# A feed-forward output product by Strassen's seven half-size products, with single input buffers

## Chip, cores, metric

The kernel runs on one core of a Trainium2 chip. The metric is the device time of one execution in microseconds (us), as the median of repeated runs. A profiled execution gives a span, from the first to the last instruction, that is some 2 us shorter than the time. The granted clock is the share of TensorE's full clock that its throttle let through, 1 at most.

## The reference

```python
# attention: per head, phi(x) = [relu(x) cos, relu(x) sin], cos and sin by position
kv  = einsum('bhsf,bhsd->bhfd', phi(k), v);   z = sum(phi(k), axis=2)
num = einsum('bhsf,bhfd->bhsd', phi(q), kv)
x   = num / (einsum('bhsf,bhf->bhs', phi(q), z)[..., None] + 1e-6)      # 8 x 8 x 576 x 64
# then, with x as (4608 tokens, 512)
h   = x @ w_in                       # 512 -> 2048
g   = h / (1 + exp(-beta * h))       # beta per column
out = g @ w_out                      # 2048 -> 512
```

## The kernel before

The 4608 tokens go in nine chunks of 512. A chunk has 32 slots. In slots 0 to 15 TensorE makes the sixteen 128-row blocks of h, transposed, and ScalarE turns each into a bfloat16 tile of g. In slots 16 to 31 TensorE makes the output product. The attention of batch c+1 is spread between the slots of chunk c, so that its VectorE and GpSimd work lies beside the matmuls. "h stage" and "output stage" below are these two halves.

```python
raw_pool = tc.tile_pool(name="raw", bufs=2)       # q, k, v of two batches
gt_pool  = tc.tile_pool(name="gt", bufs=20)

def h_bank(c, jt):                                # PSUM bank of an h block; (0, 1, 4, 5) from chunk 2 on
    ...
def h_act(c, jt):
    g_t = gt_pool.tile([P, TCH], BF16, name="g_t", tag="g_t")
    nc.scalar.activation(g_t, ps[:, h_bank(c, jt)], AF.Silu, scale=beta[:, jt : jt + 1])
    gs[c, jt] = g_t

def o_mm(c, tt, jts):                             # 128 tokens x 512 columns, 16 matmuls of N=512
    o_ps = ps[:, (2, 3, 0, 1)[tt] if c == 0 else 2 + tt % 2]
    for jt in jts:
        nc.tensor.matmul(o_ps, lhsT=gs[c, jt][:, tt * P : (tt + 1) * P],
                         rhs=wout[jt // 4][:, jt % 4, :], start=(jt == 0), stop=(jt == JT - 1))
    ...
    nc.scalar.copy(o_sb, o_ps)
    store(c, tt, o_sb)

def att_units(b):                                 # (slot, work) for batch b
    u = [(0, lambda: num_rest() if b == 2 else None),
         (0, lambda: (q_relu(b, 0), q_relu(b, 1), q_turn_dma(b), load_next())),
         (1, lambda: v_scale(b, 0)), (4, lambda: k_relu(b)), (6, lambda: v_scale(b, 1)),   # VectorE
         (7, lambda: q_tan(b, 0)), (8, lambda: q_tan(b, 1)),                               # GpSimd
         (12, lambda: (kv_mm(b, 0, 6), kv_mm(b, 1, 6), kv_take((0, 1), 6)))]
    u.append((18, lambda: (num_all(0, 4), num_all(1, 6), num_all(2, 0))))
    for t, bank in enumerate((4, 6, 0)):
        u.append((18, lambda t=t, bank=bank: (x_div(t, bank), x_turn_dma(b, 3 * t, 3 * t + 3))))
```

kv_mm is a product of k and v into bank 6 and 7, and kv_take is VectorE's copy of it. num_all(t, bank) is a third of the numerators. x_div(t, bank) is VectorE's division of them: a sum, a reciprocal and a multiplication.

## Time and profile before

| | before |
|---|---|
| time, median (range) of three runs | 294.7 us (294.2 to 294.9) |
| span | 292.4 us |
| TensorE, VectorE, ScalarE, GpSimd busy | 97%, 39%, 49%, 26% |
| granted TensorE clock | 0.998 |
| one chunk with attention, TensorE | 30.3 us: h 13.85, kv 1.2, num 1.4, output product 13.85 |

The prediction shows the lines and how they are read.

### The profile page before, as it was taken

To read this page: it belongs to the slowest core of one execution; us is meant where nothing else is said; L and a number is where in the kernel's file an instruction comes from. 1 tells how busy PE (TensorE), PEld (TensorE's weight loads), DVE (VectorE), ACT (ScalarE), POOL (GpSimd) and SP (SyncE) were. 2 spreads that over 40 slices of the span, in tenths; PEclk is the share of its full clock that TensorE was granted. 3 is DMA by queue.
4 is the path that set the end of the run, shared out by engine and by line. 5 is a ranking of instruction groups with operands and counts; after the bars stand their busy time and mean duration, and the time that the engine had idled before them with its cause. 6 is when DMAs were issued, how large, how long until landed. Compare 5 with 4: busy or idle time off the path is not lost.

```text
span 292.4 us, 7218 instructions
## 1 busy us (share of the span) xinstructions
PE 284.0 (97%) x3072; PEld 141.3 (48%) x3072; DVE 114.0 (39%) x287; ACT 142.8 (49%) x228; POOL 74.9 (26%) x89
## 2 busy tenths in 40 slices
PE   7699999999999999999999999999999999999994
PEld 6354455455445544554445444454455444444444
DVE  5889975834900392029301950086005000000000
ACT  5778856862166315721573137412760277137511
POOL 1444000643380038202650265023601210000000
PEclk9999999999999999999999999999999999999999
DMA  6999999999998089907991699139102810131033
GB/s 242 383 389 385 392 349 334 299 264 336 176 284 314 3 159 203 402 34 141 216 392 46 130 217 391 58 65 206 36 2 52 143 36 0 39 83 23 0 74 72
DMA packets 50737, 53.89 MB, mean 184 GB/s; under 512 B 31233, under 2 KB 31633, under 8 KB 50705
## 3 DMA queue, kind: packets, MB, share of 16 engines
q1 hardware_dynamic: 47744, 45.95, 53.8%
q0 software_dynamic: 2688, 7.34, 10.5%
q8 instruction: 24, 0.39, 0.5%
q10 hardware_dynamic: 272, 0.14, 0.2%
q14 instruction: 9, 0.07, 0.1%
HBM read 36.71 MB, written 9.44 MB: 158 GB/s over the span
## 4 chain that ended last, share of the span: by engine, by line
PE 92%; DMA 3%; DVE 2%; SPq 1%; issue 1%
PE ps L365 42%; PE ps L390 42%; PE ps L280 3%; DMA raw_v<-in_v_dram 3%; PE ps L259 3%; PE ps L408 1%; SPq L78 1%; DVE xs L302 1%; PE ps L229 0%; PE ps L339 0%; DVE win L108 0%; DVE rden L295 0%; DVE den L291 0%; DVE rk L189 0%; DVE vb L204 0%
## 5 line engine op out<-in xcount | busy, mean ns | idle before, releaser
L365 PE MATMUL ps<-xt,win 128*128 128x512 bf16 (+1 forms) x580 | 127.3, 378 | 0.1
L390 PE MATMUL ps<-wout,g_t 128*128 128x512 bf16 x560 | 124.4, 379 | 0.0
L372 ACT ACTIVATE g_t<-ps,beta 128x512 bf16<-128x512 f32 x144 | 98.6, 688 | 33.2 <-PE ps L365 33.2
L365 PEld LDWEIGHTS <-win 128*128 128x128 bf16 x580 | 56.0, 98 | 66.0 <-issue 0.5
L390 PEld LDWEIGHTS <-g_t 128*128 128x128 bf16 x560 | 53.7, 98 | 63.9 <-issue 0.3
L385 POOL DMA_DIRECT2D out_dram<-o_sb x56 | 35.9, 645 | 136.7 <-ACT o_sb L396 136.7
L396 ACT COPY o_sb<-ps 128x512 f32<-128x512 f32 x35 | 20.2, 588 | 98.2 <-PE ps L390 94.0
L271 DVE CAST kv<-ps 128x520 bf16<-128x520 f32 x6 | 4.2, 700 | 68.3 <-PE ps L259 68.3
L217 POOL TENSOR_TENSOR qs<-qt,tanr 128x1152 bf16<-128x1152 bf16 x12 | 28.3, 2382 | 8.2 <-DMA qt<-qb 8.2
L411 DVE COPY o_sb<-ps 128x256 f32<-128x256 f32 (+1 forms) x2 | 0.7, 358 | 62.7 <-PE ps L408 62.7
L302 DVE TENSOR_TENSOR xs<-ps,rden 128x768 bf16<-128x768 f32 (+4 forms) x26 | 22.8, 884 | 0.9 <-DVE rden L295 0.2
L291 DVE TENSOR_TENSOR den<-ps,eps 128x12 f32<-128x12 f32 (+4 forms) x26 | 4.1, 159 | 33.6 <-PE ps L280 33.5
L214 DVE TENSOR_SCALAR vb<-raw_v,cos 128x256 bf16<-128x256 f32 x63 | 17.1, 347 | 0.0
L214 DVE TENSOR_SCALAR vb<-raw_v,sin 128x256 bf16<-128x256 f32 x54 | 14.7, 349 | 0.0
L280 PEld LDWEIGHTS <-qt 64*64 64x64 bf16 x576 | 10.4, 106 | 4.9 <-issue 4.5
L259 PE MATMUL ps<-vb,rk 64*64 64x130 bf16 x576 | 10.2, 218 | 2.1 <-ACT rk L187 1.9
L280 PE MATMUL ps<-kv,qt 64*64 64x65 bf16 x576 | 11.7, 195 | 0.5 <-ACT kv L269 0.5
L189 DVE TENSOR_SCALAR qb<-raw_q 128x1152 bf16<-128x1152 f32 x16 | 11.4, 752 | 1.6 <-DMA raw_q<-in_q_dram 1.6
L259 PEld LDWEIGHTS <-rk 64*64 64x64 bf16 x576 | 8.5, 106 | 6.9 <-ACT rk L187 3.6
L280 PE MATMUL ps<-kv,qs 64*64 64x65 bf16 x576 | 11.5, 193 | 0.0
L108 DVE CAST win<-w_stage 64x512 bf16<-64x512 f32 x22 | 10.9, 493 | 1.1 <-DMA w_stage<-in_moe_w_in_dram 0.6
L189 DVE TENSOR_SCALAR rk<-raw_k 128x2304 bf16<-128x2304 f32 (+2 forms) x9 | 10.7, 1186 | 0.6 <-DMA raw_k<-in_k_dram 0.6
(59 smaller groups left out, 98.6 us busy)
## 6 DMA issues: line engine op xcount, KB each, us to landing
raw_v<-in_v_dram SPq DMA_DIRECT2D x7, 1152.0 KB, 10.4
raw_k<-in_k_dram SPq DMA_DIRECT2D x7, 1152.0 KB, 13.6
raw_q<-in_q_dram SPq DMA_DIRECT2D x7, 1152.0 KB, 7.3
out_dram<-o_sb POOLq DMA_DIRECT2D x56, 128.0 KB, 4.4
w_stage<-in_moe_w_in_dram SPq DMA_DIRECT2D x3, 1024.0 KB, 13.4
w_stage<-in_moe_w_out_dram SPq DMA_DIRECT2D x2, 1024.0 KB, 8.0
w_stage<-in_moe_w_out_dram SPq DMA_DIRECT2D x4, 512.0 KB, 12.0
out_dram<-o_sb SPq DMA_DIRECT2D x14, 128.0 KB, 2.3
```

The source lines that it names most:

```text
L108: nc.vector.tensor_copy(o, a)
L189: nc.vector.tensor_scalar(dst, src, scalar1=0.0, scalar2=None, op0=ALU.max)
L214: nc.vector.tensor_scalar(o, a, scalar1=t[:, n : n + 1], scalar2=None, op0=ALU.mult)
L217: eng.tensor_tensor(dst.rearrange("q n (g p) -> q n g p", g=2), src.rearrange("q n (g p) -> q n g p", g=2), tanr[:, n0:n1].unsqueeze(2).to ...
L259: nc.tensor.matmul(t[jj * HP : (jj + 1) * HP, g], lhsT=rk[hs, n, 2 * jp + jj, :], rhs=vb[hs, n, 2 * jp + jj].rearrange("q s e -> q (s e)") ...
L280: nc.tensor.matmul(ps[cols, bank + jj, slot * E : (slot + 1) * E], lhsT=(qt, qs)[cs][rows, jp, n, cols], rhs=kv[rows, g, jp, cs, :], start ...
L302: nc.vector.tensor_tensor(o.rearrange("q j n s d -> q j (n s) d"), nv[:, :, a:z, :, 0:D].rearrange("q j n s d -> q j (n s) d"), rden[:, :, ...
L365: nc.tensor.matmul(ps[:, h_bank(c, jt), blocks.start * 64 : blocks.stop * 64], lhsT=win[jt // 4][:, mi, (jt % 4) * P : (jt % 4 + 1) * P], ...
L372: nc.scalar.activation(g_t, ps[:, h_bank(c, jt)], AF.Silu, scale=beta[:, jt : jt + 1])
L385: eng.dma_start(out=out_v[bb, n][:, m0:m1], in_=o_sb[hf * HP : (hf + 1) * HP, m0:m1])
L390: nc.tensor.matmul(o_ps, lhsT=gs[c, jt][:, tt * P : (tt + 1) * P], rhs=wout[jt // 4][:, jt % 4, :], start=(jt == 0), stop=(jt == JT - 1))
L396: nc.scalar.copy(o_sb, o_ps)
```

## The change

The output product of chunks 1 to 8 is made by a seven-product Strassen scheme. The halves are those of tokens (256 and 256), of d_ff (even and odd 128-blocks) and of d_model. TensorE does an eighth less arithmetic in it, at matmuls of N=256 in place of 512. VectorE makes four sums of g for each chunk (S1 to S4) and four of the weights once (T1 to T4), and puts the products together. The space for these comes from single raw buffers in place of double ones, so loads are issued at other points. In chunk 1, GpSimd makes half of v's scaling. The numerators (num) move from slot 18 to the end of the h stage, so kv_take is needed three slots' matmuls (2.6 us) earlier.

```diff
-    raw_pool = ctx.enter_context(tc.tile_pool(name="raw", bufs=2))
+    raw_pool = ctx.enter_context(tc.tile_pool(name="raw", bufs=1))
...
+    T1, T2, T4 = (const.tile([P, JT // 2, HM], BF16, name=f"T{i}") for i in (1, 2, 4))
+    T3 = B12
+    S1, S2, S3, S4 = (const.tile([P, JT // 2, TCH // 2], BF16, name=f"S{i}") for i in (1, 2, 3, 4))
...
+    def g_sums(c, i0, i1):
...
+        nc.vector.tensor_tensor(s1, A21, A22, op=ALU.add)
+        nc.vector.tensor_tensor(s2, s1, A11, op=ALU.subtract)
+        nc.vector.tensor_tensor(s4, A12, s2, op=ALU.subtract)
+        nc.vector.tensor_tensor(s3, A11, A21, op=ALU.subtract)
+
+    def w_sums(i0, i1):                                   # T1 = B12-B11, T2 = B22-T1, T4 = B21-T2, T3 = B22-B12
...
+    def o_fast(c, pr, b_bank):
+        a_ps, e_ps, b_ps = (ps[:, k_, 0:HM] for k_ in (2, 3, b_bank))
...
+        def s_0():
+            prod(a_ps, g_part(0, 0), B11, True, False)     # 8 matmuls of N=256
+            nc.scalar.copy(p1, a_ps)
+        def s_1():
+            prod(b_ps, s_part(S2), T2, True, False)
+            nc.vector.tensor_tensor(u2, b_ps, p1, op=ALU.add)
...
+        def s_4():
+            prod(b_ps, s_part(S3), T3, False, False)
+            nc.vector.tensor_tensor(o2[:, HM:DM], b_ps, p15, op=ALU.add)
...
+        def s_6():
+            prod(b_ps, g_part(1, 1), T4, False, True)
+            nc.vector.tensor_tensor(o2[:, 0:HM], b_ps, p1, op=ALU.add)
...
         if slot == 24:
-            for name in "qvk":
+            for name in "vkq":
                 load_raw(2, name)
...
+            if slot in (3, 7, 11):
+                g_sums(c, slot // 2 - 1, slot // 2 + 1)
+            elif slot in (13, 15):
+                g_sums(c, slot // 2, slot // 2 + 1)
+            if c == 1 and slot in (5, 9):
+                w_sums(slot - 5, slot - 1)
+        if b < B:
+            num_all(0, 6)
+            num_all(1, 0)
+            num_all(2, 4)
+        x, y = o_fast(c, 0, 6), o_fast(c, 1, 7)            # two pairs of 128 tokens; banks 6 and 7
...
+        x[0]()
+        x_part(0)                                          # the division that reads bank 6
+        x[1]()                                             # the product that writes bank 6
+        x_part(1)
...
+        y[2]()
+        y[3]()
+        if b + 1 < B:
+            v_scale(b + 1, 0)                              # nine VectorE operations
+        y[4]()
+        y[5]()
+        y[6]()
```

x and y are the seven products of the first and the second pair of token blocks. "y4" is the fifth product of the second pair.

More of the change, by code (lines that the diff above doesn't have):

```diff
@@ L58 @@
     small = ctx.enter_context(tc.tile_pool(name="small", bufs=4))
-    gt_pool = ctx.enter_context(tc.tile_pool(name="gt", bufs=20))
+    gt_pool = ctx.enter_context(tc.tile_pool(name="gt", bufs=5))
+    part = ctx.enter_context(tc.tile_pool(name="part", bufs=2))
     osb_pool = ctx.enter_context(tc.tile_pool(name="osb", bufs=4))
@@ L82 @@
     win = [const.tile([P, MI, 512], BF16, name=f"win{i}") for i in range(4)]
-    wout = [const.tile([P, 4, DM], BF16, name=f"wout{i}") for i in range(4)]
+    wout = const.tile([P, JT, DM], BF16, name="wout")
+    HM = DM // 2
+    w_e, w_o = wout[:, 0:JT:2], wout[:, 1:JT:2]
+    B11, B12, B21, B22 = w_e[:, :, 0:HM], w_e[:, :, HM:DM], w_o[:, :, 0:HM], w_o[:, :, HM:DM]
+    T1, T2, T4 = (const.tile([P, JT // 2, HM], BF16, name=f"T{i}") for i in (1, 2, 4))
+    T3 = B12
+    S1, S2, S3, S4 = (const.tile([P, JT // 2, TCH // 2], BF16, name=f"S{i}") for i in (1, 2, 3, 4))
     w_in_v = moe_w_in.rearrange("(j p) f -> p j f", p=P)
@@ L113, in cast_out @@
         if eng == "a":
-            nc.scalar.activation(wout[i][:, jj, :], st[:, jj, :], AF.Copy, scale=rbeta[:, j : j + 1])
+            nc.scalar.activation(wout[:, j, :], st[:, jj, :], AF.Copy, scale=rbeta[:, j : j + 1])
         else:
-            nc.vector.tensor_scalar(wout[i][:, jj, :], st[:, jj, :],
+            nc.vector.tensor_scalar(wout[:, j, :], st[:, jj, :],
                                     scalar1=rbeta[:, j : j + 1], scalar2=None, op0=ALU.mult)
     GJ = [(0, 0), (0, 1), (1, 0), (1, 1)]
-    for name in "qvk":
-        for b in range(2):
-            raw_tile(b, name)
     load_raw(0, "q", 0, 2)
@@ L370, in h_act @@
     def h_act(c, jt):
-        g_t = gt_pool.tile([P, TCH], BF16, name="g_t", tag="g_t")
-        nc.scalar.activation(g_t, ps[:, h_bank(c, jt)], AF.Silu, scale=beta[:, jt : jt + 1])
-        gs[c, jt] = g_t
+        if (c, jt // 4) not in gs:
+            gs[c, jt // 4] = gt_pool.tile([P, 4, TCH], BF16, name="g_t", tag="g_t")
+        nc.scalar.activation(gs[c, jt // 4][:, jt % 4], ps[:, h_bank(c, jt)], AF.Silu, scale=beta[:, jt : jt + 1])
+    def g_sums(c, i0, i1):
+        k_ = i0 // 2
+        g_e, g_o = (gs[c, k_][:, 2 * (i0 - 2 * k_) + r : 2 * (i1 - 2 * k_) : 2] for r in range(2))
+        hf = TCH // 2
+        A11, A12, A21, A22 = g_e[:, :, 0:hf], g_o[:, :, 0:hf], g_e[:, :, hf:TCH], g_o[:, :, hf:TCH]
+        s1, s2, s3, s4 = (t[:, i0:i1] for t in (S1, S2, S3, S4))
+        nc.vector.tensor_tensor(s1, A21, A22, op=ALU.add)
[3 more added lines that the diff above has]
+    def w_sums(i0, i1):
+        a, z = slice(i0, i1), ALU.subtract
+        nc.vector.tensor_tensor(T1[:, a], B12[:, a], B11[:, a], op=z)
+        nc.vector.tensor_tensor(T2[:, a], B22[:, a], T1[:, a], op=z)
+        nc.vector.tensor_tensor(T4[:, a], B21[:, a], T2[:, a], op=z)
+        nc.vector.tensor_tensor(T3[:, a], B22[:, a], B12[:, a], op=z)
     def h_group(c, jt):
@@ L379, with store @@
     out_v = out.rearrange("(b p n) m -> b n p m", b=B, n=NQ)
-    def store(c, tt, o_sb, m0=0, m1=512, two=False):
+    def store(c, tt, o_sb):
         for hf in range(2):
             bb, n = divmod((c * TCH + tt * P) // HP + hf, NQ)
-            eng = (nc.sync, nc.scalar)[hf] if two else nc.sync if c >= 7 else nc.gpsimd
-            eng.dma_start(out=out_v[bb, n][:, m0:m1], in_=o_sb[hf * HP : (hf + 1) * HP, m0:m1])
+            eng = nc.gpsimd if c < 7 else (nc.sync, nc.scalar)[hf] if tt == 3 else nc.sync
+            eng.dma_start(out=out_v[bb, n], in_=o_sb[hf * HP : (hf + 1) * HP])
     def o_mm(c, tt, jts):
@@ L389, in o_mm @@
         for jt in jts:
-            nc.tensor.matmul(o_ps, lhsT=gs[c, jt][:, tt * P : (tt + 1) * P],
-                             rhs=wout[jt // 4][:, jt % 4, :],
+            nc.tensor.matmul(o_ps, lhsT=gs[c, jt // 4][:, jt % 4, tt * P : (tt + 1) * P],
+                             rhs=wout[:, jt, :],
                              start=(jt == 0), stop=(jt == JT - 1))
@@ L400, in o_part, with prod, g_part, at @@
         o_mm(c, tt, range(4 * part, 4 * part + 4))
-    def o_last(c, tt):
-        o_sb = osb_pool.tile([P, DM], FP32, name="o_sb", tag="o_sb")
-        for i, (m0, m1) in enumerate(((0, 256), (256, 384), (384, 512))):
-            o_ps = ps[:, 4 + i, 0 : m1 - m0]
-            for jt in range(JT):
-                nc.tensor.matmul(o_ps, lhsT=gs[c, jt][:, tt * P : (tt + 1) * P],
-                                 rhs=wout[jt // 4][:, jt % 4, m0:m1],
-                                 start=(jt == 0), stop=(jt == JT - 1))
-            (nc.scalar.copy if i == 1 else nc.vector.tensor_copy)(o_sb[:, m0:m1], o_ps)
-            store(c, tt, o_sb, m0, m1, two=True)
+    def o_fast(c, pr, b_bank):
+        a_ps, e_ps, b_ps = (ps[:, k_, 0:HM] for k_ in (2, 3, b_bank))
+        tok = slice(pr * P, (pr + 1) * P)
+        def prod(dst, left, right, start, stop):
+            for i in range(JT // 2):
+                nc.tensor.matmul(dst, lhsT=left(i), rhs=right[:, i], start=start and i == 0,
+                                 stop=stop and i == JT // 2 - 1, skip_group_check=True)
+        def g_part(r, hf):
+            def at(i):
+                jt = 2 * i + r
+                return gs[c, jt // 4][:, jt % 4, hf * (TCH // 2) + pr * P : hf * (TCH // 2) + (pr + 1) * P]
+            return at
+        def s_part(t):
+            return lambda i: t[:, i, tok]
+        o1 = osb_pool.tile([P, DM], FP32, name="o_sb", tag="o_sb")
+        o2 = osb_pool.tile([P, DM], FP32, name="o_sb", tag="o_sb")
+        p1 = part.tile([P, HM], FP32, name="p1", tag="p1")
+        p15 = part.tile([P, HM], FP32, name="p15", tag="p15")
+        u2 = part.tile([P, HM], FP32, name="u2", tag="u2")
+        def s_0():
[4 more added lines that the diff above has]
+            nc.vector.tensor_tensor(u2, b_ps, p1, op=ALU.add)
+        def s_2():
+            prod(e_ps, s_part(S1), T1, True, False)
+            nc.vector.tensor_tensor(p15, e_ps, p1, op=ALU.add)
+        def s_3():
+            prod(a_ps, g_part(1, 0), B21, False, True)
+            nc.scalar.copy(o1[:, 0:HM], a_ps)
+        def s_4():
+            prod(b_ps, s_part(S3), T3, False, False)
+            nc.vector.tensor_tensor(o2[:, HM:DM], b_ps, p15, op=ALU.add)
+        def s_5():
+            prod(e_ps, s_part(S4), B22, False, True)
+            nc.vector.tensor_tensor(o1[:, HM:DM], e_ps, u2, op=ALU.add)
+            store(c, pr, o1)
+        def s_6():
+            prod(b_ps, g_part(1, 1), T4, False, True)
+            nc.vector.tensor_tensor(o2[:, 0:HM], b_ps, p1, op=ALU.add)
+            store(c, pr + 2, o2)
+        return s_0, s_1, s_2, s_3, s_4, s_5, s_6
@@ L564, in num_rest, with att_q, att_h, v_second @@
         x_turn_dma(1, 7, NQ)
-    def att_units(b):
-        def load_next():
-            for name in "qvk":
-                if b + 1 < B:
-                    load_raw(b + 1, name)
-        u = [
-            (0, lambda: num_rest() if b == 2 else None),
-            (0, lambda: (q_relu(b, 0), q_relu(b, 1), q_turn_dma(b), load_next())),
-            (1, lambda: v_scale(b, 0)),
-            (4, lambda: k_relu(b)),
-            (6, lambda: v_scale(b, 1)),
-            (7, lambda: q_tan(b, 0)),
-            (8, lambda: q_tan(b, 1)),
-            (12, lambda: (kv_mm(b, 0, 6), kv_mm(b, 1, 6), kv_take((0, 1), 6))),
-        ]
-        u.append((18, lambda: (num_all(0, 4), num_all(1, 6), num_all(2, 0))))
-        for t, bank in enumerate((4, 6, 0)):
-            u.append((18, lambda t=t, bank=bank: (x_div(t, bank), x_turn_dma(b, 3 * t, 3 * t + 3))))
-        return sorted(u, key=lambda x: x[0])
+    def att_q(b):
+        q_relu(b, 0)
+        q_relu(b, 1)
+        q_turn_dma(b)
+        if b + 1 < B:
+            load_raw(b + 1, "q")
+    def att_h(b):
+        def v_second():
+            if b == 2:
+                for jp in range(2):
+                    v_scale(b, 1, jp, eng="pool")
+            else:
+                v_scale(b, 1)
+            if b + 1 < B:
+                load_raw(b + 1, "v")
+        def k_all():
+            k_relu(b)
+            if b + 1 < B:
+                load_raw(b + 1, "k")
+        return {
+            0: lambda: (num_rest(), att_q(2), v_scale(2, 0)) if b == 2 else None,
+            1: k_all,
+            2: v_second,
+            7: lambda: q_tan(b, 0),
+            8: lambda: q_tan(b, 1),
+            12: lambda: (kv_mm(b, 0, 6), kv_mm(b, 1, 6), kv_take((0, 1), 6)),
+        }
     for slot in range(32):
@@ L602 @@
         if slot == 24:
-            for name in "qvk":
+            for name in "vkq":
                 load_raw(2, name)
@@ L607, with x_part @@
     for c in range(1, NTC):
-        units = att_units(c + 1) if c + 1 < B else []
-        for slot in range(32):
-            if slot < 16:
-                h_group(c, slot)
-            elif c == NTC - 1 and slot >= 28:
-                if slot == 28:
-                    o_last(c, 3)
-            else:
-                o_part(c, (slot - 16) // 4, slot % 4)
-            while units and units[0][0] <= slot:
-                units.pop(0)[1]()
+        b = c + 1
+        units = att_h(b) if b < B else {}
+        for slot in range(16):
+            h_group(c, slot)
+            if slot in units:
+                units[slot]()
+            if slot in (3, 7, 11):
[9 more added lines that the diff above has]
+        x, y = o_fast(c, 0, 6), o_fast(c, 1, 7)
+        banks = (6, 0, 4)
+        def x_part(t):
+            if b < B:
+                x_div(t, banks[t])
+                x_turn_dma(b, 3 * t, 3 * t + 3)
+        x[0]()
+        x_part(0)
+        x[1]()
+        x_part(1)
+        x[2]()
+        x_part(2)
+        x[3]()
+        x[4]()
+        x[5]()
+        if b + 1 < B:
+            att_q(b + 1)
+        y[0]()
+        x[6]()
+        y[1]()
+        y[2]()
+        y[3]()
+        if b + 1 < B:
+            v_scale(b + 1, 0)
+        y[4]()
+        y[5]()
+        y[6]()
 _INS = ['q', 'k', 'v', 'moe_w_in', 'moe_w_out', 'moe_beta']
```

## The prediction

> **What bounds the kernel now.** I began with the page's first two parts. TensorE is busy 97% of the span at full clock, and no other engine is over half.
>
> ```profile
> PE 284.0 (97%) x3072; PEld 141.3 (48%) x3072; DVE 114.0 (39%) x287; ACT 142.8 (49%) x228; POOL 74.9 (26%) x89
> ...
> PEclk9999999999999999999999999999999999999999
> ```
>
> Next the chain of waits that ended last and the table of groups: two matmul lines share the span, the product into d_ff (L365) and the output product (L390), and neither has idle time ahead of it. Per matmul the cost is busy time over count (124.4 / 560 = 0.222 us), not the 379 ns mean, because matmuls overlap.
>
> ```profile
> PE 92%; DMA 3%; DVE 2%; SPq 1%; issue 1%
> PE ps L365 42%; PE ps L390 42%; PE ps L280 3%; DMA raw_v<-in_v_dram 3%; PE ps L259 3%; PE ps L408 1%; SPq L78 1%; DVE xs L302 1%; PE ps L229 0%; PE ps L339 0%; DVE win L108 0%; DVE rden L295 0%; DVE den L291 0%; DVE rk L189 0%; DVE vb L204
> ...
> L390 PE MATMUL ps<-wout,g_t 128*128 128x512 bf16 x560 | 124.4, 379 | 0.0
> ```
>
> Then the timeline of TensorE over one chunk (c=2), columns start, length, engine, line, operation, count:
>
> ```profile
> 81.36 11.39 PE L365 MATMUL ps<-xt,win 128*128 128x512 bf16 x52
> 92.68 1.22 PE L259 MATMUL ps<-vb,rk 64*64 64x130 bf16 x72
> 93.82 2.76 PE L365 MATMUL ps<-xt,win 128*128 128x512 bf16 x12
> 96.42 2.75 PE L390 MATMUL ps<-wout,g_t 128*128 128x512 bf16 x12
> 100.47 11.40 PE L390 MATMUL ps<-wout,g_t 128*128 128x512 bf16 x52
> ```
>
> One start to the next gives 0.2165 us a matmul, so 13.85 us each for the h stage and the output stage (64 matmuls each); 1.2 us for kv and 1.4 us for num; 30.3 us in all, without a hole. Every microsecond taken from TensorE counts, and every microsecond for which the new code makes it wait counts too.
>
> VectorE in the same chunk, where the output stage runs:
>
> ```profile
> 99.82 0.17 DVE L291 TENSOR_TENSOR den<-ps,eps 128x12 f32<-128x12 f32 x1 [5.18 <-PE ps L280]
> 100.03 0.23 DVE L295 RECIPROCAL rden<-den 128x12 f32<-128x12 f32 x1
> 100.29 0.96 DVE L302 TENSOR_TENSOR xs<-ps,rden 128x768 bf16<-128x768 f32 x1
> ...
> 103.83 1.42 DVE L189 TENSOR_SCALAR qb<-raw_q 128x1152 bf16<-128x1152 f32 x2
> 105.16 2.45 DVE L214 TENSOR_SCALAR vb<-raw_v,cos 128x256 bf16<-128x256 f32 x9
> ```
>
> Here nothing on TensorE waits for these. The h stage of this chunk has 0.7 us of VectorE work in 15.2 us, the output stage 11.2 us in 15.2 (busy time by windows).
>
> **What the skill says.** "TensorE: Matmul & The Clock Gate", Back-to-back issue gap: N/2.4 + 2.5 ns warm, so 109 ns at N=256. The trace agrees at 512 (216.5), and the split last tile shows the narrow ones: its first 16 matmuls at N=256 start at 284.90 and the copy of their sum starts 286.90, which leaves about 110 ns each after the 0.25 us tail that every consumer shows; its 48 take 3.70 us in all, so weight loads hide even at N=128. The slower sustained 81 ns at N=128 in the same section is not seen. "VectorE: DVE Perf Modes", perf-mode tier table: tensor_tensor of bf16 in SBUF runs at two elements a cycle, of fp32 at one. The trace has only the one-per-cycle form: 957 ns for 768 columns and 425 for 256, thus 158 ns plus 1.04 ns a column. "SBUF — State Buffer", Who interferes with whom: a VectorE operation with two SBUF inputs and a GpSimd one that reads SBUF exclude each other. No run here shows it, since VectorE is idle while q_tan runs. "TensorE: Matmul & The Clock Gate", What's actually happening: about 3.4 us of idleness halves the clock; the trace has no such gap after the start.
>
> **The change, part by part.** Take t=0 where TensorE issues the last h matmul's successor.
>
> *Removed on TensorE.* 64 x 0.2165 = 13.85 us become 7 products x 2 token pairs x 8 = 112 matmuls of N=256, 112 x 0.1093 = 12.24 us. Gain 1.61 us a chunk, x8 = **-12.9 us**. It is 11.6% of the product and not 12.5%, owing to the 2.5 ns a matmul.
>
> *Added on VectorE.* Estimates from the rows and the tier table: a sum over 512 bf16 columns 158 + 267 = 425 ns, over 256 291 ns, over 1024 691 ns; a dependent successor starts 35 ns after (den to rden in the trace), an independent one 80 ns before the end. g_sums is then 3 x 1.72 + 2 x 1.19 = 7.5 us a chunk, the ten PSUM combinations 10 x 0.42 = 4.2 us, w_sums 2 x 2.8 = 5.6 us once. VectorE goes from 11.9 to about 23.6 of some 30 us: not the bound on average, so what matters is the order in its queue.
>
> *Wait 1, chunks 1 to 6.* The second product writes bank 6, which num_all(0) filled and x_div(0) must have read. x_div(0) stands behind g_sums of slot 15, and that waits for the last silu: 0.26 to start + 0.69 = 0.95. Sums end at 0.95 + 0.05 + 1.19 = 2.2. x_div's chain, 0.20 + 0.27 + 0.96, ends at 3.65, released 3.7. TensorE is there after num 1.4 and the first product 0.87, at 2.3. Stall 1.4 us, x6 = **+8.5 us**.
>
> *Wait 2, chunks 1 to 5.* v_scale of the next batch (2.45 us, nine operations) stands ahead of y4's combination, and y6 accumulates into the same bank 7. Let y2 end its issue at T: p15 is done at T+0.67, v_scale at T+3.0, y4's combination at T+3.4; y6 would start at T+2.6. Stall 0.85 us, x5 = **+4.3 us**.
>
> *Chunk 1.* VectorE's h-stage queue, from the start of the stage: 2.7 (num_rest's division) + 1.35 (q relu) + 2.4 (v_scale) + 1.3 (k relu) + 3 x 1.72 + 5.6 + 0.7 (kv_take) = 19.1 us to kv_take, since w_sums lies ahead of it. The stage on TensorE is 15.5 us, and num_all cannot start without kv_take: stall 3.6 us if GpSimd does not disturb. GpSimd has four SBUF operations here (two v halves at 2.1 us, two q_tan at 2.4, together 9 us), mostly alongside VectorE's sums; I charge a quarter to a third, 2.5 us. The gap could pass 3.4 us, so 0.7 us for a lowered clock. **+6.8 us**.
>
> *Small.* Chunks 7 and 8 have no division; S2's last slice is ready about when it is needed (0.1 us each). The tail ends with a 0.42 us combination and 128 KB stores instead of 0.29 us and 32 KB ones (2.3 against about 2 us to landing): +0.4. Other queueing, q_tan beside VectorE in chunks 2 to 6: +0.5. **+1.1 us**.
>
> *Moved.* Single raw buffers: each load is issued right after its relu or scale and has most of a 30 us chunk, against 7 to 17 us to landing. Batch 2's q, now last of three, can go out at about 41 us, when batch 1's relu ends, and is wanted at 53 us: hidden. ScalarE loses 4 copies of 0.59 and gains 4 half-wide ones; not on the path.
>
> Sum: -12.9 + 8.5 + 4.3 + 6.8 + 1.1 = +7.8, 302.5 us. The ordering of the new code looks deliberate (g_sums split at slots 13 and 15, part of v to GpSimd in chunk 1), so I take 1 us off for stalls that I may have drawn too long: **301.5 us**.
>
> **Rivals.** (a) *The gain arrives.* If the divisions and sums were all hidden, 282 to 284 us. For it: average VectorE load near 80%. Against it: the three queue orders above, each built from measured durations. If VectorE's sums were much cheaper than 291 to 691 ns, wait 1 would lose at most 1 us and chunk 1 some 6: about 290. (b) *Exclusion between VectorE and GpSimd is complete.* Chunk 1's stall grows towards 12 us with a cold clock; with small additions in later chunks, about 310. The skill speaks for it, no trace does. (c) *The sums run at one element a cycle*, 691 ns for 512: wait 1 grows by about 0.5 us x 6, chunk 1 by over 6 us: also near 310. (d) *Narrow matmuls don't hide their weight loads*: each 10 ns costs 112 x 8 x 0.01 = 9 us; the split tile speaks against. (e) *Loads of the single buffers come late*: a stall of VectorE by raw_q or raw_v; the 20 us of slack speaks against.
>
> **Range and chances.** Low end, 293: waits 1 and 2 cut by half, chunk 1 without disturbance. High end, 310: (b) or (c). Within 2% is 288.8 to 300.6; my figure lies just past it and the deliberate ordering pulls back, so slower 0.50, same 0.41, faster 0.09. Predicted 301.5 us, range 293 to 310.
>
> **What would show it.** Output products of 128x256, 896 of them, with about 98 us busy in place of 124; TensorE below 95% busy; its idle time put down to VectorE: xs of the division (L302 before) ahead of the second product by about 1.4 us in six chunks, the y4 combination ahead of y6 by 0.85 in five, kv_take ahead of num_all in chunk 1 by 3 to 7 us. VectorE near 210 us busy (114 + 8 x (7.5 + 4.2) + 5.6 - 2.4). I am wrong if the second product is not held by the division, if the bf16 sums measure far from 291 and 425 ns, or if the idle time stands before other matmuls or behind a DMA.

## More of the kernel before

Of the other runs one was slow and is left out of its ratio.

## The result

| | before | after |
|---|---|---|
| time, median (range) | 294.8 us (294.2 to 295.2) | 306.4 us (305.8 to 306.7) |
| ratio (95%) | | 1.040 (1.038 to 1.042) |
| span | 292.4 us | 304.0 us |

A ratio is the mean time of one kernel's fast runs over that of the other's fast runs of the same rounds, so it isn't quite the ratio of the medians. The change made the kernel slower by 4%. The prediction said 301.5 us, within 293 to 310, with "slower" the likeliest class.

The page of the changed kernel, the same lines as before:

```profile
PE 275.3 (91%) x3420; PEld 179.6 (59%) x3424; DVE 229.5 (75%) x524; ACT 136.2 (45%) x228; POOL 81.2 (27%) x91
...
PEclk9999999997599999999999999999999999999999
```

TensorE has 8.7 us less work and 28.7 us without any, where before it had 8.4. VectorE's work has doubled. The clock has a dent at a quarter of the span. TensorE's waits (engine, line, releaser; us in total, times, longest):

```profile
PE ps L284 <- DVE kv L275: 11.0, 1, 11.0
PE ps L263 <- DVE rk L193: 3.2, 3, 1.9
PE ps L432 <- DVE xs L306: 3.1, 4, 1.0
PE ps L432 <- DVE o_sb L468: 2.9, 5, 0.6
PE ps L284 <- issue: 1.5, 2, 0.8
```

L284 is num, L275 kv_take, L263 kv, L432 the seven products, L306 the division's multiplication and L468 y4's combination. The idle time is counted from a modelled end that lies 0.16 us after a matmul has let the next one start, so from issue to issue each wait is that much longer. Now the timeline of TensorE, chunk 1 and then chunk 2:

```profile
64.99 2.76 PE L369 MATMUL ps<-xt,win 128*128 128x512 bf16 x12
78.77 0.27 PE L284 MATMUL ps<-kv,qt 64*64 64x65 bf16 x4 [11.02 <-DVE kv L275]
...
94.69 11.39 PE L369 MATMUL ps<-xt,win 128*128 128x512 bf16 x52
...
111.20 1.05 PE L432 MATMUL ps<-wout,g_t 128*128 128x256 bf16 x8
113.21 1.91 PE L432 MATMUL ps<-T,S 128*128 128x256 bf16 x16 [0.96 <-DVE xs L306]
...
121.94 1.91 PE L432 MATMUL ps<-wout,S 128*128 128x256 bf16 x16
124.44 1.03 PE L432 MATMUL ps<-T,g_t 128*128 128x256 bf16 x8 [0.59 <-DVE o_sb L468]
125.31 11.39 PE L369 MATMUL ps<-xt,win 128*128 128x512 bf16 x52
```

From the starts of L369 (L365 before) one reads the length of each chunk, and the whole difference of the spans:

| stretch | before, us | after, us | difference |
|---|---|---|---|
| up to chunk 1 | 50.53 | 50.02 | -0.5 |
| chunk 1 | 30.83 | 44.67 | +13.8 |
| chunks 2 to 5, each | 30.34 to 30.36 | 30.61 to 30.73 | +1.2 in all |
| chunk 6 | 30.35 | 29.87 | -0.5 |
| chunks 7 and 8, each | 27.6 | 26.05 | -3.2 in all |
| behind the last matmul's issue | 4.0 | 4.8 | +0.8 |
| span | 292.4 | 304.0 | +11.6 |

Where there is no attention the change gives what it should, 1.6 us a chunk. In chunks 2 to 5 two small waits (in chunks 4 and 5 also a hole of another kind, see experiment 8) take it back, and chunk 1 alone loses more than all the chunks could win. This is VectorE's queue in chunk 1 (start, length, engine, line, operation, count, idle before and its end), with GpSimd's in the fence behind it:

```profile
55.83 4.32 DVE L193 TENSOR_SCALAR qb<-raw_q 128x1152 bf16<-128x1152 f32 x2 [3.08 <-DMA raw_q<-in_q_dram]
60.07 2.44 DVE L218 TENSOR_SCALAR vb<-raw_v,cos 128x256 bf16<-128x256 f32 x9
...
65.29 2.87 DVE L393 TENSOR_TENSOR T<-wout 128x1024 bf16<-128x1024 bf16 x1
68.19 2.75 DVE L394 TENSOR_TENSOR T<-wout,T 128x1024 bf16<-128x1024 bf16 x1
70.97 0.69 DVE L395 TENSOR_TENSOR T<-wout,T 128x1024 bf16<-128x1024 bf16 x1
...
78.02 0.69 DVE L275 CAST kv<-ps 128x520 bf16<-128x520 f32 x1
```

```profile
54.84 4.70 POOL L208 TENSOR_TENSOR vb<-raw_v,sin 128x1152 bf16<-128x1152 f32 x2
65.06 5.33 POOL L221 TENSOR_TENSOR qs<-qt,tanr 128x1152 bf16<-128x1152 bf16 x2 [5.52 <-DMA qt<-qb]
```

kv_take (L275) ends at 78.7. The h stage was through at 67.6. Two relus take 4.32 us here and 1.42 in every other chunk. The first two weight sums take 2.87 and 2.75 us, a third like them 0.69. In each case one or two GpSimd operations run beside them (v's scaling until 59.5, q_tan from 65.06), and in front of the relus VectorE waits 3.08 us for q. That made three suspects for chunk 1: the weight sums in the queue, GpSimd, and q's load.

### The profile page after: what moved, and what is told of

Read it like the earlier page. It is cut to its first block, busy times and chain, and to the rows that moved or that the text cites. A ratio compares the mean times of both kernels' runs of the same rounds, so it can differ in the third digit from the quotient of the medians.

```text
span 304.0 us, 8116 instructions
## 1 busy us (share of the span) xinstructions
PE 275.3 (91%) x3420; PEld 179.6 (59%) x3424; DVE 229.5 (75%) x524; ACT 136.2 (45%) x228; POOL 81.2 (27%) x91
## 4 chain that ended last, share of the span: by engine, by line
PE 58%; DVE 23%; DMA 16%; issue 1%; ACT 1%; SPq 1%; DVEq 0%
PE ps L432 28%; PE ps L369 27%; DMA raw_q<-in_q_dram 11%; DVE vb L218 7%; DMA w_stage<-in_moe_w_in_dram 4%; DVE qb L193 2%; PE ps L263 2%; DVE S L387 1%; DVE S L388 1%; DVE xs L306 1%; PE ps L284 1%; DVE win L115 1%; DVE T L394 1%; DVE T L393 1%; DVE S L386 1%
## 5 line engine op out<-in xcount | busy, mean ns | idle before, releaser
L369 PE MATMUL ps<-xt,win 128*128 128x512 bf16 (+1 forms) x580 | 127.4, 378 | 0.1
L377 ACT ACTIVATE g_t<-ps,beta 128x512 bf16<-128x512 f32 x144 | 98.6, 688 | 58.3 <-PE ps L369 56.2
L369 PEld LDWEIGHTS <-win 128*128 128x128 bf16 x580 | 55.9, 98 | 64.6 <-issue 0.5
L432 PEld LDWEIGHTS <-S 128*128 128x128 bf16 x512 | 50.0, 98 | 9.9 <-issue 3.9
L432 PEld LDWEIGHTS <-g_t 128*128 128x128 bf16 x384 | 37.4, 99 | 9.0 <-issue 3.8
L432 PE MATMUL ps<-wout,g_t 128*128 128x256 bf16 x256 | 34.0, 277 | 0.0
L432 PE MATMUL ps<-T,S 128*128 128x256 bf16 x256 | 30.5, 272 | 3.1 <-DVE xs L306 3.1
L221 POOL TENSOR_TENSOR qs<-qt,tanr 128x1152 bf16<-128x1152 bf16 x12 | 29.5, 2483 | 6.8 <-DMA qt<-qb 6.7
L218 DVE TENSOR_SCALAR vb<-raw_v,sin 128x256 bf16<-128x256 f32 x45 | 30.6, 756 | 0.0
L432 PE MATMUL ps<-wout,S 128*128 128x256 bf16 x256 | 30.6, 273 | 0.0
L386 DVE TENSOR_TENSOR S<-g_t 128x512 bf16<-128x512 bf16 (+1 forms) x40 | 14.7, 367 | 19.6 <-ACT g_t L377 19.4
L284 PE MATMUL ps<-kv,qt 64*64 64x65 bf16 x576 | 12.7, 200 | 13.0 <-DVE kv L275 11.0
L306 DVE TENSOR_TENSOR xs<-ps,rden 128x768 bf16<-128x768 f32 (+4 forms) x26 | 22.8, 884 | 0.8
L284 PEld LDWEIGHTS <-qt 64*64 64x64 bf16 x576 | 11.4, 112 | 17.6 <-issue 17.2
L432 PE MATMUL ps<-T,g_t 128*128 128x256 bf16 x128 | 16.6, 272 | 2.9 <-DVE o_sb L468 2.9
L387 DVE TENSOR_TENSOR S<-S,g_t 128x512 bf16<-128x512 bf16 (+1 forms) x40 | 17.0, 425 | 1.4
L388 DVE TENSOR_TENSOR S<-g_t,S 128x512 bf16<-128x512 bf16 (+1 forms) x40 | 16.9, 423 | 1.4
```

Source lines behind the costliest of these rows:

```text
L218: nc.vector.tensor_scalar(o, a, scalar1=t[:, n : n + 1], scalar2=None, op0=ALU.mult)
L221: eng.tensor_tensor(dst.rearrange("q n (g p) -> q n g p", g=2), src.rearrange("q n (g p) -> q n g p", g=2), tanr[:, n0:n1].unsqueeze(2).to ...
L284: nc.tensor.matmul(ps[cols, bank + jj, slot * E : (slot + 1) * E], lhsT=(qt, qs)[cs][rows, jp, n, cols], rhs=kv[rows, g, jp, cs, :], start ...
L306: nc.vector.tensor_tensor(o.rearrange("q j n s d -> q j (n s) d"), nv[:, :, a:z, :, 0:D].rearrange("q j n s d -> q j (n s) d"), rden[:, :, ...
L369: nc.tensor.matmul(ps[:, h_bank(c, jt), blocks.start * 64 : blocks.stop * 64], lhsT=win[jt // 4][:, mi, (jt % 4) * P : (jt % 4 + 1) * P], ...
L377: nc.scalar.activation(gs[c, jt // 4][:, jt % 4], ps[:, h_bank(c, jt)], AF.Silu, scale=beta[:, jt : jt + 1])
```

## The experiments

Each kernel is the changed one with one edit, unless said otherwise. The times to compare are 306.4 us after and 294 to 295 us before. The runs fell in more than one session, in which the kernel before took 294.1 to 294.8 us, so a difference of under 1 us is not read.

### 1. The division ahead of the last sums

The wait ahead of the second product should be due to x_div(0), which stands behind the sums of slot 15 in VectorE's queue.

```diff
+            if slot == 14 and b < B:
+                num_all(0, 6)
+                x_div(0, 6)
...
-            num_all(0, 6)
```

> One edit to the changed kernel: the first third of num and its division (the one that reads bank 6) go ahead of the sums of slot 15 in VectorE's queue. Theory (queue order): the gap ahead of the second output product, 1.14 us from issue to issue in chunks 2 to 5 and the like in 6, is gone, the chunk period falls from 30.6 to about 29.5 us, and the time from 306.4 to about 301 (5 x 1.1); chunk 1 stays, its stall stands ahead of num. Rival (the second product is held just as long by its own operand S2, the sum of slot 15): the gap only shrinks to 0.5 or so, time 303 to 304. Second rival (VectorE has no slack at all, so the wait only moves to another product): no change.

Measured: 306.6 us (306.2 to 307.1), ratio to before 1.041. There was no change, as the second rival had it, but not for its reason. TensorE's waits in this kernel no longer name L306:

```profile
PE ps L284 <- DVE kv L275: 12.8, 3, 11.9
PE ps L432 <- DVE o_sb L468: 2.9, 5, 0.6
PE ps L284 <- ACT g_t L377: 1.2, 5, 0.2
```

The wait aimed at is gone: in chunk 2 the second product follows the first without a hole. Two others came with the edit, since it moved TensorE's work too. num now meets kv_take in three chunks in place of one, and its last third comes right behind the last h block, whose bank the silu is still reading (0.2 us each time by the modelled end). In chunk 1 the last h block also stood behind the long wait, and the chunk grew from 44.7 to 46.5 us. Chunk 2 became 30.5 and chunk 3 30.1 us. The run shows the cause of the wait, and that this is not the way to remove it.

### 2. The sums behind the division

The second try leaves TensorE's order alone and swaps only VectorE's.

```diff
-            elif slot in (13, 15):
+            elif slot == 13 or slot == 15 and b >= B:
...
         x_part(0)
+        if b < B:
+            g_sums(c, 7, 8)
         x[1]()
```

> The wait ahead of the second output product, tried again without moving TensorE's work: num stays where it is, only the sums of slot 15 go behind the first division in VectorE's queue (chunks 1 to 6). The first try removed that wait but put num ahead of kv_take and ran its last third into the bank of the last silu. Theory (queue order): the 1.13 us go and nothing takes their place, period of chunks 2 to 5 from 30.6 to 29.5, time down by 5 to 6 us to about 301. Rival (the sum S2 then comes too late for the second product): a gap of 0.5 us or more stays ahead of it, time 303 or more.

Measured: 302.2 us (301.6 to 302.9), ratio 1.027, so 4.2 us less. TensorE in chunk 2:

```profile
111.62 1.05 PE L432 MATMUL ps<-wout,g_t 128*128 128x256 bf16 x8
112.50 1.91 PE L432 MATMUL ps<-T,S 128*128 128x256 bf16 x16
```

The gap is gone, and chunks 2 and 3 take 29.50 us each, 1.12 less than in the changed kernel. Chunk 4 takes 30.3, with 0.63 us ahead of num for which the trace names no releaser. The changed kernel had such pieces too (0.8 and 0.7 us in chunks 4 and 5, "issue" in its list of waits), but there they lay in front of the wait for the division and cost little. More of them comes in experiment 8.

### 3. v's scaling split

```diff
-            v_scale(b + 1, 0)
+            v_scale(b + 1, 0, n1=5)
         y[4]()
         y[5]()
+        if b + 1 < B:
+            v_scale(b + 1, 0, n0=5)
```

> One edit to the changed kernel: of the nine v_scale operations that stand ahead of the fifth product's combination of the second token pair, four are moved behind it and the next. Theory (queue order): the last product of chunks 1 to 5 no longer waits 0.75 us from issue to issue, time down by 5 x 0.75 = 3.7 us to 302.6. Rival (the wait is given back: VectorE enters the next h stage equally late, and the sums or kv_take pay for it): the last product starts on time but the period stays 30.6 and the time 306.

Measured: 303.0 us (302.6 to 303.5), ratio 1.028, 3.4 us less. No product waits for L468 any more and chunk 2 takes 29.87 us, 0.75 less. The theory holds to its number, and nothing of it was lost again elsewhere in VectorE's queue. Chunk 4 alone took longer, 31.1 us: 2.15 us of it are a hole ahead of num without a releaser, of the kind of experiment 8.

### 4. The weight sums out of chunk 1

```diff
-            if c == 1 and slot in (5, 9):
-                w_sums(slot - 5, slot - 1)
...
+        if slot == 31:                      # end of chunk 0; T3 in space that the weight staging has left
...
+            w_sums(0, 4)
+            w_sums(4, 8)
```

> One edit to the changed kernel: the weight sums (T1 to T4, T3 in its own space that the weight staging has left) are made at the end of chunk 0, in VectorE's idle time before batch 2's q lands, and not between the sums of chunk 1. Theory (they stand ahead of kv_take in the queue, with 9.5 us as measured, 5.6 as worked out): TensorE's 11.0 us before num in chunk 1 shrink to 1 to 2 us, the clock doesn't fall, time down by 10 to 11 us to about 295.5. Rival (chunk 1 is late mainly by q's load and by GpSimd beside VectorE, and these delays fall on other operations when the weight sums are gone): 5 to 6 us, 300 to 301.

Measured: 301.4 us (301.0 to 303.8), ratio 1.025, so 5.0 us less and not 10 to 11: the rival's number. VectorE's queue shows why:

```profile
55.55 4.71 DVE L193 TENSOR_SCALAR qb<-raw_q 128x1152 bf16<-128x1152 f32 x2
...
65.39 2.60 DVE L386 TENSOR_TENSOR S<-g_t 128x512 bf16<-128x512 bf16 x1
68.02 2.49 DVE L387 TENSOR_TENSOR S<-S,g_t 128x512 bf16<-128x512 bf16 x1
70.55 0.42 DVE L388 TENSOR_TENSOR S<-g_t,S 128x512 bf16<-128x512 bf16 x1
```

The 4.2 us that q_tan on GpSimd cost the weight sums now fall on two sums of g, 2.60 and 2.49 us in place of 0.42. Here the cost of a collision followed GpSimd's operation, not the VectorE operation that met it. The weight sums' own share was 5.2 us of kv_take's delay (it ends at 73.5 in place of 78.7).

### 5. GpSimd's part of chunk 1 on VectorE

```diff
-            if b == 2:                       # v_second: half of v's scaling by GpSimd
+            if False:
...
-        tan_mul(nc.gpsimd, qs[:, jp], qt[:, jp], 0, NQ)
+        tan_mul(nc.vector if b == 2 else nc.gpsimd, qs[:, jp], qt[:, jp], 0, NQ)
```

> One edit to the changed kernel: batch 2's second half of v and its two q_tan go from GpSimd to VectorE, so that in chunk 1 GpSimd does nothing but stores. It gives VectorE 2.45 + 2 x 1.36 = 5.2 us more work ahead of kv_take. Theory (GpSimd's SBUF operations hold up VectorE for their whole length): the two q relus fall from 4.32 to 1.42 us and the two slow weight sums from 2.87 and 2.75 to 0.69 each, 7.0 us in all, so kv_take comes 1.8 us earlier in spite of the added work: time about 304.5. Rival (those operations are slow for another reason, their inputs or the transfers): they stay slow and kv_take comes 5.2 us later, time about 311.5.

Measured: 304.8 us (302.9 to 306.0), ratio 1.036. The theory said 304.5 and the rival 311.5. VectorE's queue:

```profile
56.02 1.43 DVE L193 TENSOR_SCALAR qb<-raw_q 128x1152 bf16<-128x1152 f32 x2 [2.77 <-DMA raw_q<-in_q_dram]
...
64.95 0.68 DVE L393 TENSOR_TENSOR T<-wout 128x1024 bf16<-128x1024 bf16 x1
65.67 0.69 DVE L394 TENSOR_TENSOR T<-wout,T 128x1024 bf16<-128x1024 bf16 x1
```

All three slow groups are back at their plain durations, and kv_take ends at 76.7 in place of 78.7 although VectorE has taken over 5.2 us of work. So in chunk 1 the work given to GpSimd relieved VectorE of nothing.

### 6. q's buffer double again

```diff
+    raw_q_pool = ctx.enter_context(tc.tile_pool(name="raw_q", bufs=2))   # S1 to S4 move to the staging space
...
+            pool = raw_q_pool if name == "q" else raw_pool
```

> One edit to the changed kernel: q's raw buffer is double again (space from the weight staging, where S1 to S4 now lie), so that batch 2's q is loaded without waiting for batch 1's relu. Theory (the single buffer delayed q): VectorE's 3.1 us wait for q in chunk 1 is gone or nearly, everything behind it in the queue moves up, time down by 3 us to 303.4. Rival (the transfers are limited by the queue and the order v, k, q, not by the buffer): q lands when it did, no change. Second rival (the 3 us are won but GpSimd's v operations now collide with other VectorE operations for as long): little change although the wait for q is gone.

Measured: 307.3 us (306.7 to 309.8), ratio 1.045: no gain. The wait for q is 2.73 us in place of 3.08. The transfers' queue of this kernel:

```profile
38.76 0.46 SPq L81 DMA_DIRECT2D raw_k<-in_k_dram  x1
40.27 2.39 SPq L81 DMA_DIRECT2D raw_q<-in_q_dram  x1
```

In the changed kernel v's load was issued at 36.80, k's at 37.39 and q's at 40.40; here v's goes out at 38.16, since this trace runs some 1.3 us later. Counted from v's issue, the second buffer lets q's load go 1.5 us sooner (2.1 us behind v's in place of 3.6), but q lands only 0.5 us sooner (18.5 in place of 19.0), as the third load in the row. So the single buffer of q cost at most 0.5 us. What remains is the order. The kernel before had q first and k third: issued at about the same times, its q landed at 49.1 and its k at 56.2. Experiment 8 loads q first and has no wait for it, but with other edits too; the order was not tested alone.

### 7. Chunk 1 with the plain product

```diff
+            if c == 1:
+                continue                     # no sums of g in chunk 1
...
+        if c == 1:                           # the plain product, the divisions and, at slot 8, the weight sums
+            for slot in range(16):
+                o_part(c, slot // 4, slot % 4)
...
+                elif slot == 8:
+                    w_sums(0, 4)
+                    w_sums(4, 8)
```

> Chunk 1 keeps the plain output product; the seven products begin with chunk 2. The weight sums are made in chunk 1's output stage, where VectorE has room (T3 in its own space). Theory (chunk 1's loss is VectorE's queue ahead of kv_take: sums of g and of weights, the collisions with GpSimd and the late q): without both kinds of sums only 2 to 4 us of waiting for k's relu and for q_tan stay, chunk 1 takes 34 to 35 us in place of 44.7, time about 296.5. Rival (late q and GpSimd alone make chunk 1 late): chunk 1 stays above 39 us, time over 300.

Measured: 299.1 us (297.4 to 300.3), ratio 1.016. Chunk 1 takes 35.9 us in place of 44.7, and the clock stays up (0.996). Chunks 2 to 4 are as in the changed kernel; chunks 5 and 6 take 0.7 us longer each, with holes of 1.8 and 1.6 us without a releaser, which is about half of what the time lies above the 296.5 us expected. What remains in chunk 1 are 1.95 us ahead of kv (k's relu, behind the late q), 1.85 ahead of num (q_tan) and 0.8 without a releaser.

### 8. All together, and where the rest went

The combined kernel has the edits of 2, 3 and 7, q doubled and loaded first, and v's second half in chunk 1 on VectorE.

> All that has been learned in one kernel: chunk 1 plain with the weight sums in its output stage, its v on VectorE, q double-buffered and loaded first; the slot 15 sums behind the first division; v_scale split 5 and 4. Theory: chunk 1 takes 31 to 32 us, chunks 2 to 6 about 28.8 (30.34 less 1.6), chunks 7 and 8 26.04 as before: 292.4 + 0.5 - 7 x 1.6 + 0.4 of tail gives a span of 282, a time of 284 to 285, below both kernels. Rival (VectorE, then some 92% busy in such a chunk, becomes the bound by its load and its collisions with q_tan): chunks of 29.5 to 30, time 288 to 291.

Measured: 292.4 us (290.6 to 295.6; the slowest left out), ratio 0.992 (0.988 to 0.996). It beats both kernels, the one before by 0.8% ("same" at the limit of 2%), but by far less than worked out. Chunk 2 takes 28.75 us, 1.6 less than before, as it should. Chunks 3 to 5 take 29.5, 30.1 and 31.1 us, and chunk 6 30.7. TensorE:

```profile
132.08 0.83 PE L433 MATMUL ps<-T,w_stage 128*128 128x256 bf16 x6 [0.61 <-issue]
...
161.22 1.80 PE L433 MATMUL ps<-T,w_stage 128*128 128x256 bf16 x15 [1.19 <-issue]
...
191.43 0.94 PE L433 MATMUL ps<-wout,g_t 128*128 128x256 bf16 x7 [1.91 <-issue]
```

Each hole is in the middle of a product, whose other matmuls had gone through, so neither a bank nor an operand held it. The rival named VectorE, and VectorE isn't it. "issue" means that the trace names no releaser. With one in chunk 1 and one in chunk 6 it is 6.9 us. In chunks 3 to 6, one block of the instruction queue (27 blocks with 0.44 MB on the changed kernel's page, 16 KB each) lands in or just behind num, up to 3 us ahead of the hole's end. The Trainium skill, "Runtime: NRT & Kernel Launch", Instruction fetch mechanics, says that instructions come in 16 KiB blocks of 256 and that crossing a boundary is "mostly hidden". num and the seven products issue 288 and 224 instructions in 1.4 and 12.2 us; the plain product issued 128 in 13.85. So two kernels were run that differ from the combined one only in the number of instructions ahead of everything: the warm-up at the start, with the same array time.

```diff
-    warm_pe(58, 48)
+    warm_pe(26, 107)     # 64 instructions fewer; the other kernel: warm_pe(90, 31), 64 more
```

> The combined kernel (292.4 us) lost 6.9 us of TensorE time, in pieces of 0.6 to 1.9 us in chunks 1 and 3 to 6, for which the trace names no releaser; each comes 0.3 to 3 us after one block of the instruction queue (16 KB, 256 instructions) has landed in num, which issues 288 TensorE instructions in 1.4 us. A chunk has 784 of them, 3 x 256 + 16, and the pieces grow from chunk to chunk. This kernel differs in nothing but the warm-up at the start: 26 matmuls of width 107 in place of 58 of width 48, the same array time with 64 fewer instructions, so that every later block boundary falls 64 instructions later. Theory (TensorE waits for its instructions): the pieces move and shrink, to 1 to 4 us in all, time 287 to 290. Rival (the pieces belong to the schedule of data, say a bank or a semaphore that the trace doesn't show): they stay where they are, 292.

Measured: 292.1 us (291.1 to 294.3), ratio 0.990. The holes moved: 1.39 and 2.42 us ahead of chunk 1 and 2.51 in chunk 3, with none in chunks 4 to 6. Their sum, 6.3 us, hardly fell, and the time did not. The profiled run is the slowest of the five (294.3 us; the others 291.1 to 292.2). Behind the hole in chunk 3 the granted clock fell too (0.76 and 0.68 up to 140 us), so that this chunk took 33.1 us.

> The same as the run before in the other direction: 90 warm-up matmuls of width 31, 64 more instructions than the combined kernel, boundaries 64 instructions earlier. Theory (TensorE waits for its instructions): the pieces move again, and are not those of the combined kernel; by their growth with an earlier boundary they should be larger or begin in chunk 2, 7 us or more in all, time 292 to 296. Rival (schedule of data): as in the combined kernel, 292.

Measured: 290.5 us (288.5 to 291.5), ratio 0.988 (0.984 to 0.992). The holes moved too, to 1.25 us in chunk 1, 1.03 in chunk 2 and 0.30 in chunk 5, 2.6 us in all: fewer where I had expected more. (A wait of 1.73 us in chunk 0, which the trace puts down to a GpSimd cast, is not counted, though it too stands on the grid described below.) In the profiled run, the fastest of the four, chunks 3, 4 and 6 take 28.75 us. TensorE from chunk 3 to 4:

```profile
114.33 11.39 PE L370 MATMUL ps<-xt,win 128*128 128x512 bf16 x52
...
130.84 1.05 PE L433 MATMUL ps<-wout,g_t 128*128 128x256 bf16 x8
131.73 1.91 PE L433 MATMUL ps<-T,w_stage 128*128 128x256 bf16 x16
...
143.08 3.19 PE L370 MATMUL ps<-xt,win 128*128 128x512 bf16 x14
```

That the holes move when only the number of earlier instructions changes speaks for the supply of instructions. By itself it would not settle the matter, since there is one trace of each kernel and the time of one kernel varies by 2 to 3 us from run to run. The records of the kept traces settle it, though no view of the profile prints what is needed. Number TensorE's instructions in order (weight loads, matmuls and the semaphore instructions among them), and look at the first matmul behind every hole named "issue". There are 24 of over 0.12 us in nine traces, not counting one of 0.16 us in the changed kernel's trace where matmul records are missing. All 24 stand at a multiple of 256 plus 193 or 194, and all end 1.3 to 1.6 us after a 16 KB instruction block has landed. The waits with a named releaser stand anywhere on this grid. Some of the 24:

| trace | hole ends at, us | its length, us | number of the matmul behind it | from the last block's landing to the hole's end, us |
|---|---|---|---|---|
| changed kernel | 172.97 | 0.79 | 4289 = 16 x 256 + 193 | 1.33 |
| experiment 3 | 172.24 | 2.15 | 4289 = 16 x 256 + 193 | 1.27 |
| combined | 191.43 | 1.91 | 5058 = 19 x 256 + 194 | 1.54 |
| 64 fewer | 134.27 | 2.51 | 3266 = 12 x 256 + 194 | 1.60 |
| 64 more | 101.91 | 1.03 | 2753 = 10 x 256 + 193 | 1.35 |

So TensorE stood at the border of a block that had not come in time; no other account of the holes fits both regularities, though the records don't name the engine that a block was for. Where a hole can be is set by the count of instructions. How long it is, and whether it shows at all, differs between kernels with the same TensorE instructions (0.79 and 2.15 us above, none in experiment 5). So the expectation that holes grow with an earlier border had no basis; what sets their length was not tested. This last kernel has the lowest median, 1.2% below the kernel before, but its interval overlaps that of the combined kernel.

## Why the prediction was right, and where it was off

**TensorE's gain.** Worked out: 12.24 us for 112 matmuls, 1.6 us a chunk. Measured: chunk 8's seven products take from 287.00 to 299.2, 12.2 us, and chunks 7 and 8 gain 1.6 each. Rival (d), weight loads that don't hide behind narrow matmuls, falls. N/2.4 + 2.5 of the skill's "TensorE: Matmul & The Clock Gate" holds at N=256.

**VectorE's durations.** Worked out: 425, 291 and 691 ns for 512, 256 and 1024 columns, on the tier table of "VectorE: DVE Perf Modes". Measured undisturbed: 0.42, 0.29 and 0.69 us. Rival (c) falls.

**Wait 1.** Predicted 1.4 us in each of six chunks. It is the wait I named, with the releaser I named (experiments 1 and 2), at 1.1 us (113.21 less 111.20 less the product's 0.87) in chunks 2, 3 and 6. A hole named "issue" ahead of it covered it in chunk 4 and most of it in chunk 5 (0.19 us left), and the slow clock covered it in chunk 1. Experiment 5, whose trace has no such holes, shows it in chunks 4 and 5 as well (0.89 and 0.78 us by the modelled end).

**Wait 2.** Predicted 0.85 us in five chunks, measured 0.75. Experiment 3 removed it alone.

**Chunk 1.** This is the term that was mis-sized. The sum had 3.6 us for the queue to kv_take, 2.5 for GpSimd and 0.7 for the clock, 6.8 in all; together with the gain and waits 1 and 2 that made the chunk 7.5 us longer. It became 13.8 us longer. kv_take was worked out to end 19.1 us into the chunk and ended at 28.7. The difference is q's late landing (3.1 us, put aside as rival (e) with "hidden") and the collisions with GpSimd, 2.9 us at the relus and 4.2 at the weight sums, where I had charged 2.5 for all; the rest of the queue ran 0.6 us shorter than worked out. On TensorE this became 11.2 us ahead of num and 2.1 ahead of kv, from issue to issue. The page "SBUF — State Buffer", Who interferes with whom, says that one blocks the other fully, and experiment 5 shows it: its rule should have been taken whole, as rival (b) had it. The prediction also named only operations with two inputs in SBUF; the relus and v's scalings have one, and collided as well. The same collisions occur in later chunks (nine scalings take 6.7 to 8.0 us in place of 2.45 in four of them, two sums of g 2.5 and 2.6 in place of 0.42 in the fifth), and there VectorE's slack hides them from num, as I had it. All collisions together are some 30 us, more than the distance between 210 us of VectorE work as predicted and 229.5 as measured: without them it would be about 200, so that sum was 10 us too high.

**q's load.** I found it hidden because it goes out at 41 us and is wanted at 53, without asking how long a third load in the row takes. It went out at 40.4 and VectorE got it at 55.8, 15.4 us later; 15.4 is also the longest of q's loads in this trace. The change gave q the last place. The single buffer wasn't the cause (experiment 6).

**The clock.** Expected if the gap passed 3.4 us; it was 11.0. (In the kernel with 64 instructions fewer it fell behind a hole of 2.5 us, so 3.4 us was no safe limit.) The granted clock falls to 0.5 to 0.7 in two slices, num takes 2.15 us in place of 1.4 and the first product 1.66 in place of 0.87, which is 1.5 us where I had 0.7.

**Small terms.** The tail grew by 0.8 us and not 0.4. The holes named "issue" weren't foreseen. The 1 us that I took off because the order looked deliberate was not due.

**Where luck helped.** Chunk 1 came out 6.3 us worse than the sum. Chunks 2 to 6 came out 1.7 us better (0.7 us longer in all, where gain and waits gave 2.4), since both waits were drawn somewhat too long. That the time lies 4.9 us and not 6 or more from the prediction owes something to these errors of opposite sign.

## What to carry to other kernels

When work moves from a full engine to one that is 40% busy on average, write down the receiver's queue in order for the first, a middle and the last stage, because each operation waits for everything ahead of it: here 1.6 us a chunk was won, 1.9 us were given back by two places in the order, and the one stage with extra set-up work lost 14. In these traces VectorE and GpSimd did not add up while both read SBUF, so work moved to GpSimd relieved VectorE only while VectorE was idle or read PSUM alone (kv_take beside q_tan took its plain 0.70 us in the kernel before). Move one engine's order at a time: the same wait came back in another form when TensorE's order was changed and vanished when VectorE's was. And where TensorE idles for no named reason, number its instructions: holes at equal distances on a grid of 256 pointed to the supply of instructions.

## What the Trainium skill lacked or had wrong

- "SBUF — State Buffer", Who interferes with whom: right, with its rule that the order of issue decides who blocks. q_tan began at 65.06 and the weight sum at 65.29, and the sum took 2.87 us in place of 0.69. What the page doesn't spell out is the outcome when short operations meet long ones: VectorE paid nearly all. Two q_tan took 4.7 us alone and 4.8 to 5.3 beside VectorE, while nine VectorE scalings beside them took 6.7 us or more in place of 2.45.
- "VectorE: DVE Perf Modes", perf-mode tier table: right. bf16 sums in SBUF measured 0.42, 0.29 and 0.69 us for 512, 256 and 1024 columns.
- "TensorE: Matmul & The Clock Gate", Back-to-back issue gap: the formula given for an isolated matmul holds for a stream with a weight load ahead of every matmul (216.5 ns at N=512, 109 at N=256). The same section's sustained 131 ns at N=512 was seen nowhere here.
- "Runtime: NRT & Kernel Launch", Instruction fetch mechanics: "mostly hidden". In the combined kernel 6.9 us of TensorE idle time came in five pieces. They stood at block borders, as all 24 such holes in nine traces did, and ended 1.3 to 1.6 us after a block had landed. Around a dense stretch of small matmuls up to 2.5 us showed at one border.
- No page that I read says how long a load waits behind others of its own queue. Of three 1.15 MB loads issued at 36.8, 37.4 and 40.4 us, the first landed at 48.6, the second at 52.5 and the third at 55.8, 15.4 us after its issue; the median for that tensor was 7.7.
